# One loop of chunk pairs for all MLP passes, seven products in passes 2 to 4, Gelu in one ScalarE function, three raw weight buffers

## The chip, the core and the metric

The kernel runs on one core of a Trainium2 chip. TensorE multiplies into PSUM, VectorE (DVE in rows), ScalarE (ACT) and GpSimd (POOL) work on SBUF and PSUM, SyncE (SP) issues transfers. The metric is the time of one execution on the device in microseconds (us). A run's profile has a span, from the first to the last instruction; the time is a few us longer.

## What is computed

Clustered attention, then two MLP layers over its output, in float32 accuracy:

```python
mask = q_assign[:, :, :, None] == k_assign[:, :, None, :]
scores = np.where(mask, scale * np.matmul(q, k.transpose(0, 1, 3, 2)), -1000000000.0)
attn = softmax(scores)                      # B, H, S, D = 2, 8, 768, 64
x = np.matmul(attn, v).transpose(0, 2, 1, 3).reshape(B * S, H * D)     # 1536 x 512
h = x @ moe_w_in                            # layer 0: 512 -> 2048
x = (h * (1.0 / (1.0 + np.exp(-1.702 * h)))) @ moe_w_out
r = np.maximum(x @ moe2_w_in, 0.0)          # layer 1
out = (r * r) @ moe2_w_out
```

The weights come as float64 and are read as pairs of 32-bit words.

## The kernel before

Float32 products are made from two parts of each operand, a high part rounded to `F32R` and the rest as a low part; three products of parts (high by high, high by low, low by high) make one. A "part" step is a ScalarE copy to `F32R` and a subtract.

Attention comes first and isn't touched, apart from where decoded weights lie. Its end makes the parts `xs` of the first batch's rows and the hidden product of chunk 0.

The MLP runs in four passes: layer 0 on batch 0 and batch 1, layer 1 on batch 0 and batch 1. The 2048 hidden units are 16 chunks of 128 (`fc`). A chunk's hidden product has 24 matmuls, its second product (`second`, L719) adds into six PSUM tiles `y` and has 24 matmuls in layer 0 and 18 in layer 1, interleaved one chunk or pair later as `pend`.

- Pass 1 (L893 to L950) goes chunk by chunk, with 512 and 256 columns (`HALVES`). Within chunk `fc` it decodes the weights of chunk `fc + 1`: ScalarE takes the magnitude (`magnitude`, L81), VectorE does four steps (`decode`, L87: clamp, shift and mask, sign, low word), then ScalarE copies the high part and POOL subtracts the low one (`parts`, L105). The decoded first matrix is also stored to DRAM (`keep`, L123) for pass 2.
- Passes 2 to 4 (L960 to L1107) go by pairs of chunks, "slots" `q`. The first three slots of pass 2 (`NC = 3`) are plain: 48 matmuls of 384 columns for the hidden part. All others use seven products in place of eight, 42 matmuls (`product`, L836), with sums of rows (`Combos`) and of weights (`Weights.sums`). The weights are read back from DRAM two chunks at a time.
- In passes 2 and 3 the slots also decode layer 1's weights: `COUNTS` says how many tiles (of 32 `tasks`) a slot takes, `step` does one of five steps, `fetch` loads the next raw tile, `absolute` is the magnitude.
- Layer 0's activation is Sigmoid on ScalarE, a multiply on VectorE, a copy to the high part on ScalarE and a subtract on VectorE (`gate`, L701; `split`, L696; `low`, L712). Layer 1's is Relu and Square.
- The last slot of a pass makes five of seven parts of the next pass's rows (`nxt.part`), the first slot of a pass the other two, and empties `y` (`finish`).

The order on each engine is the order of the code (`manual_schedule`); a wait holds all that stands behind it on its engine. Raw weights have two buffers (`wraw`), decoded ones two (`tmpw`).

Of the kernel before, what the change touches and what calls it, by code (L numbers as in the profile page):

```python
# [34 lines left out]
def tile_kernel(ctx, tc, q, k, v, cent, w_in1, w_out1, w_in2, w_out2, cw_cols, out):  # L35
# [21 lines left out]
    wraw_p = ctx.enter_context(tc.tile_pool(name="wraw", bufs=2))  # L57
    tmp_p = ctx.enter_context(tc.tile_pool(name="tmpw", bufs=2))
# [13 lines left out]
    def w_dma(w, fc, first):  # L72
        raw = wraw_p.tile([P, DM, 2], U32, tag="raw64", name="raw64")
# [7 lines left out]
    def magnitude(raw):  # L81

        t = tmp_p.tile([P, raw.shape[1]], U32, tag="dec", name="dec")
        nc.scalar.activation(f32(t), f32(raw)[:, :, 1], ACTF.Abs)  # L84
        return raw, t
# [30 lines left out]
    def w_tiles(fc):  # L116

        wi = (wx_p if fc % 2 == 0 else wp_b[1]).tile([P, 2, KD * P], F32R, tag="wx", name="wi")
        return (wi[:, 0, :], wi[:, 1, :]) + out_tiles(fc)

# [13 lines left out]
    def hidden(xs, w, i, ph=None, span=slice(0, 3 * KD)):  # L134

        ih, il = w[0], w[1]
        a, n = HALVES[i]
        if ph is None:
            ph = duo.tile([P, n], F32, tag=("sd", "pt0")[i], name="ph")

        terms = [(w, kc, z) for w, z in ((ih, 0), (ih, 1), (il, 0)) for kc in range(KD)]
        for j, (w, kc, z) in list(enumerate(terms))[span]:
            nc.tensor.matmul(ph, w[:, kc * P:(kc + 1) * P], xs[kc][z][:, a:a + n],  # L143
# [4 lines left out]
    def attention(actx):  # L148
# [44 lines left out]
        raw = [w_dma(w_in1, 0, True), w_dma(w_out1, 0, False)]  # L193
# [332 lines left out]
        w1 = w_tiles(0)  # L526
# [28 lines left out]
        xs, mags = [], []  # L555
        none = lambda: None
# [33 lines left out]
        for t in range(-LEAD, NTILE):  # L590
# [43 lines left out]
            for i, at in enumerate((t + LEAD - GT, t + LEAD - 2 * GT, t + LEAD - 3 * GT, t + LEAD - 4 * GT)):  # L634
                fc, m = divmod(i, 2)
                if at == 0:
                    mags.append(magnitude(raw[m]))
                if 0 < at < 5:
                    decode(*mags[i], steps=(at - 1,), inside=i == 3)
                if at == 5:  # L640
# [15 lines left out]
        nc.scalar.activation(tiny.tile([P, 1], F32, name="warm", bufs=1), identF[:, 0:1], ACTF.Sigmoid)  # L656
# [3 lines left out]
        raw[0] = w_dma(w_in1, 3, True)  # L660
# [18 lines left out]
    xb_p = ctx.enter_context(tc.tile_pool(name="xb", bufs=6))  # L679
# [4 lines left out]
    NP = KF // 2  # L684
    h = m_p.tile([P, 2, S], F32, name="h")
    s = m_p.tile([P, S], F32, name="s")
    wt = m_p.tile([P, 4, 2 * P], F32, name="wt")
    p5 = m_p.tile([P, QB], F32, name="p5")
# [7 lines left out]
    def split(g, src, at=slice(0, S)):  # L696
        gh, gl = g
        nc.scalar.copy(gh[:, at], src[:, at])
        nc.vector.tensor_sub(gl[:, at], src[:, at], f32(gh[:, at]))
# [5 lines left out]
    def total(layer, dst, ps, other):  # L705

        if layer == 0:
            nc.vector.tensor_tensor(out=dst, in0=ps, in1=other, op=ALU.add)
        else:
            nc.vector._custom_dve(TENSOR_ADD_SAT, out=dst, in0=ps, in1=other, s0=TOP, s1=0.0)  # L710
# [4 lines left out]
    def squared(g, c, at):  # L715
        nc.scalar.activation(g[0][:, at], h[:, c, at], ACTF.Square)  # L716
        nc.scalar.activation(h[:, c, at], h[:, c, at], ACTF.Square)  # L717

    def second(layer, y, chunks):  # L719

        def unit(m, i):
            (gh, gl), (oh, ol), fc = chunks[i]
            if layer == 0:
                cs = slice(m * P, (m + 1) * P)
                yb = y[4 + m // 2][:, m % 2 * 256:m % 2 * 256 + 256]
                for z, (l, r) in enumerate(((oh, gl), (ol, gh), (oh, gh))):
                    first, last = fc == 0 and z == 0, fc == KF - 1 and z == 2
# [4 lines left out]
            else:  # L732
                for z, (l, r) in enumerate(((gh, oh), (gh, ol), (gl, oh))):
                    nc.tensor.matmul(y[m], l[:, m * P:(m + 1) * P], r,  # L734
                                     start=(fc == 0 and z == 0), stop=(fc == KF - 1 and z == 2))

        units = [(m, i) for m in range(6 if layer else KD) for i in range(len(chunks))]
# [3 lines left out]
    def finish(layer, y, b, k, copies=(nc.scalar.copy, nc.vector.tensor_copy)):  # L741
# [403 lines left out]
```

## Time and profile before

| | us |
|---|---|
| time, median of 3 runs | 802.42 (801.85 to 803.82) |
| profiled execution, its own time | 803.57 |
| its span | 800.6 |
| TensorE busy | 778.6 |
| VectorE busy | 645.2 |
| ScalarE busy | 507.5 |
| GpSimd busy | 163.7 |

Busy time is time with an instruction in the engine. Matmuls are pipelined: a matmul's listed time is longer than its distance to the next one, so pace is read from starts. A row of the timeline names its start, length, engine, line, operation, tiles out<-in, shape and count, and in brackets the idle time before it with what ended it.

### The profile page before, as it was taken

Reading aid. Unit: us, or ns where it says so; the run is one execution under the profiler, and the core shown is the slowest. Engines: PE = TensorE matmul, PEld = TensorE weight load, DVE = VectorE, ACT = ScalarE, POOL = GpSimd, SP = SyncE. Lnnn points to the kernel's source line nnn. Section 1 sums busy time; section 2 is a strip of 40 time slices with the busy share of each in tenths; the row PEclk is TensorE's granted clock in tenths of the full one; section 3 lists DMA queues with packets and bytes.
Section 4 is the critical chain, followed back from the end, with each engine's and each line's share of the span. In section 5 each row is a group of like instructions: output and inputs, shape, how many; then the busy total and the mean of one; then the engine's idle time right before and its main releaser. Section 6 shows DMA issues by size and latency. Waiting matters only on the chain.

```text
span 800.6 us, 12533 instructions
## 1 busy us (share of the span) xinstructions
PE 778.6 (97%) x4520; PEld 697.6 (87%) x4521; DVE 645.2 (81%) x1122; ACT 507.5 (63%) x1052; POOL 163.7 (20%) x153
## 2 busy tenths in 40 slices
PE   8999999999999999999989899999999999999997
PEld 5889989999989887788889799988999988898896
DVE  7899999998898799899879889988787887445532
ACT  5798888988978644454465554557565567445542
POOL 1435535545436234233300000000000000000000
PEclk9999999999999999999999999999999999999999
DMA  8242543532311344454546433321334301200002
GB/s 232 85 133 69 162 114 85 139 89 68 85 21 38 89 139 151 132 158 145 185 122 204 148 94 118 97 88 63 123 97 141 131 27 66 94 27 26 27 1 79
DMA packets 48477, 81.87 MB, mean 102 GB/s; under 512 B 5120, under 2 KB 32544, under 8 KB 48416
## 3 DMA queue, kind: packets, MB, share of 16 engines
q1 hardware_dynamic: 43232, 73.96, 30.8%
q10 hardware_dynamic: 5184, 7.12, 2.7%
q8 instruction: 35, 0.57, 0.3%
q14 instruction: 26, 0.21, 0.1%
HBM read 58.76 MB, written 11.58 MB: 88 GB/s over the span
## 4 chain that ended last, share of the span: by engine, by line
PE 58%; DVE 17%; DMA 12%; ACT 8%; issue 2%; POOL 1%; ACTq 0%; SPq 0%; POOLq 0%; DVEq 0%
PE ps L840 16%; PE y L734 15%; DMA raw<-in_moe_w_in_dram 6%; PE pa L456 5%; PE pt L431 5%; DMA raw<-in_moe_w_out_dram 3%; PE y L728 3%; PE ps L407 3%; DVE el L444 3%; PE ps L408 2%; DVE dec L98 2%; DVE nm L413 2%; DVE dec L101 2%; ACT dec L84 2%; DMA wst<-dec 2%
## 5 line engine op out<-in xcount | busy, mean ns | idle before, releaser
L444 DVE TENSOR_TENSOR el<-pt,eh 128x384 fp32r<-128x384 f32 x192 | 97.5, 549 | 8.0 <-ACT eh L441 7.4
L413 DVE TENSOR_REDUCE nm<-ps 128x1 f32<-128x768 f32 x96 | 91.2, 950 | 12.6 <-PE ps L408 11.8
L422 ACT ACTIVATE e<-ps,nm 128x768 f32<-128x768 f32 x96 | 88.7, 924 | 14.0 <-DVE rows L488 6.7
L441 ACT CAST eh<-pt 128x384 fp32r<-128x384 f32 x192 | 84.0, 497 | 9.9 <-PE pt L431 8.8
L431 PE MATMUL pt<-identF,e 128*128 128x128 f32 x576 | 81.8, 276 | 2.2 <-DVE el L444 1.6
L840 PE MATMUL ps<-x,wxh 128*128 128x384 f32 x336 | 73.6, 341 | 3.7 <-ACT wxh L812 2.7
L84 ACT ACTIVATE dec<-raw 128x512 f32<-128x512 f32 x64 | 43.1, 674 | 53.3 <-DMA raw<-in_moe_w_out_dram 27.1
L716 ACT ACTIVATE gh<-h 128x384 fp32r<-128x384 f32 (+1 forms) x48 | 30.4, 633 | 72.5 <-DVE h L710 72.0
L734 PE MATMUL y<-oh,gl 128*128 128x512 f32 x192 | 75.9, 395 | 0.0
L734 PE MATMUL y<-ol,gh 128*128 128x512 f32 x192 | 75.8, 395 | 0.0
L734 PE MATMUL y<-oh,gh 128*128 128x512 f32 x192 | 74.6, 389 | 0.0
L431 PEld LDWEIGHTS pt<-identF,e 128*128 128x128 f32 x576 | 64.4, 140 | 7.8 <-DVE el L444 6.9
L407 PE MATMUL ps<-k,q 80*128 80x512 f32 x192 | 70.2, 366 | 0.9 <-ACT k L374 0.5
L98 DVE SCALAR_TENSOR_TENSOR dec<-raw,dec 128x512 uint32<-128x512 uint32 x64 | 70.0, 1093 | 0.8
L713 DVE TENSOR_TENSOR gl<-h,gh 128x384 fp32r<-128x384 f32 (+1 forms) x75 | 50.0, 667 | 22.9 <-ACT h L717 19.6
L840 PEld LDWEIGHTS ps<-x,wxh 128*128 128x128 f32 x336 | 60.2, 191 | 7.7 <-ACT wxh L812 3.0
L408 PE MATMUL ps<-k,q 128*128 128x512 f32 x192 | 61.3, 340 | 0.0
L143 PE MATMUL ph<-xh,wi 128*128 128x512 f32 (+1 forms) x256 | 53.7, 342 | 3.7 <-ACT wi L107 3.4
L840 PE MATMUL ps<-x,wyh 128*128 128x384 f32 x252 | 54.7, 337 | 0.2 <-DVE x L791 0.2
L143 PEld LDWEIGHTS ph<-xh,wi 128*128 128x128 f32 x256 | 41.4, 189 | 12.1 <-ACT wi L107 6.5
L728 PE MATMUL y<-gl,oh 128*128 128x512 f32 x128 | 50.4, 394 | 0.9 <-DVE gl L713 0.9
L728 PE MATMUL y<-gh,ol 128*128 128x512 f32 x128 | 50.8, 397 | 0.0
(173 smaller groups left out, 1915.0 us busy)
## 6 DMA issues: line engine op xcount, KB each, us to landing
raw<-in_moe_w_in_dram SPq DMA_DIRECT2D x32, 512.0 KB, 4.0
raw<-in_moe_w_out_dram SPq DMA_DIRECT2D x32, 512.0 KB, 3.4
wb<-wst SPq DMA_DIRECT2D x24, 512.0 KB, 4.8
wst<-dec SPq DMA_DIRECT2D x32, 256.0 KB, 2.4
k<-k SPq DMA_DIRECT2D x16, 192.0 KB, 3.1
q<-q SPq DMA_DIRECT2D x16, 192.0 KB, 3.2
rr<-row SPq DMA_DIRECT2D x16, 192.0 KB, 3.5
out_dram<-o SPq DMA_DIRECT2D x12, 256.0 KB, 2.1
```

What stands on the lines that cost most here:

```text
L98: nc.vector.scalar_tensor_tensor(out=t, in0=high, scalar=0xC0000000, in1=t, op0=ALU.bitwise_and, op1=ALU.bitwise_or)
L143: nc.tensor.matmul(ph, w[:, kc * P:(kc + 1) * P], xs[kc][z][:, a:a + n], start=(j == 0), stop=(j == len(terms) - 1))
L407: nc.tensor.matmul(ps[:, a:a + n], q1[0:K1, qs], k1[0:K1, a:a + n], start=True, stop=False)
L408: nc.tensor.matmul(ps[:, a:a + n], q2[:, qs], k2[:, a:a + n], start=False, stop=True)
L413: nc.vector.tensor_reduce(out=nm, in_=live["s", t][:, 0:S], op=ALU.max, axis=AX, negate=True)
L422: nc.scalar.activation(e, live["s", t][:, 0:S], ACTF.Exp, bias=live.pop(("nm", t)), accum_out=sums[:, s:s + 1])
L431: nc.tensor.transpose(pt[:, i], e[:, kc * P:(kc + 1) * P], identF)
L441: nc.scalar.copy(place("eh", t, u), live["pt", t, u])
L444: nc.vector.tensor_tensor(out=place("el", t, u), in0=live.pop(("pt", t, u)), in1=f32(place("eh", t, u)), op=ALU.subtract)
L728: nc.tensor.matmul(y[m], l[:, cs], r[:, 0:512], start=first, stop=last)
L734: nc.tensor.matmul(y[m], l[:, m * P:(m + 1) * P], r, start=(fc == 0 and z == 0), stop=(fc == KF - 1 and z == 2))
L840: nc.tensor.matmul(ps, w[a][:, wi, kc * P:(kc + 1) * P], x[z][:, kc, :], start=start and j == kc == 0, stop=j == 2 and kc == 1, skip_group ...
```

## The change

- All passes run in one loop over 32 slots (layer, batch, pair). The eight slots of pass 1 are plain pairs (`PLAIN`) with two halves of 384 columns; slots 8 to 31 all use seven products. Slot 0 takes chunks 0 and 1, whose second hidden product stands in two `y` tiles.
- Layer 0's activation is `Gelu_apprx_sigmoid` on ScalarE, called twice, once into the high part and once into `h` (`active`); VectorE's multiply and the tiles `s` and `p5` are gone.
- The tasks now hold layer 0's remaining weights too (27 `near` tiles in pass 1), then layer 1's 32. Their subtracts are VectorE's; POOL has none of them any more. The magnitude may be taken one tile ahead in pass 1, into the weight tile of a later pair or into `room`.
- Raw weights have three buffers, taken in turn; the separate decoded tiles are gone. The last normalization (`last_norm`, on POOL) moves to the start of the MLP.
- The second product goes chunk by chunk within a pair (`order`), the later chunk first in passes 2 to 4, except in the last pair of a pass.

```diff
-    wraw_p = ctx.enter_context(tc.tile_pool(name="wraw", bufs=2))
-    tmp_p = ctx.enter_context(tc.tile_pool(name="tmpw", bufs=2))
+    wraw_p = ctx.enter_context(tc.tile_pool(name="wraw", bufs=1))
+    tmp_p = ctx.enter_context(tc.tile_pool(name="tmpw", bufs=1))
...
+    def raw_tile(at):
+        return (wraw_p, wraw_p, tmp_p)[at].tile([P, DM, 2], U32, tag=f"raw{at}", name="raw64")
...
-    def gate(dst, src, tmp):
-        nc.scalar.activation(tmp, src, ACTF.Sigmoid, scale=1.702)
-        nc.vector.tensor_mul(dst, src, tmp)
...
+    def active(layer, g, c, at, src=None):
+        if src is None:
+            src = h[:, c, at]
+        elif layer == 1:
+            nc.scalar.activation(h[:, c, at], src, ACTF.Relu)
+            src = h[:, c, at]
+        of = ACTF.Square if layer else ACTF.Gelu_apprx_sigmoid
+        nc.scalar.activation(g[0][:, at], src, of)
+        nc.scalar.activation(h[:, c, at], src, of)
...
-    NC = 3
-    COUNTS = (3, 4, 3, 2, 2, 2, 2, 0, 1, 2, 2, 2, 2, 2, 2, 1)
+    PLAIN = range(NP)
+    COUNTS = (2, 4, 4, 4, 4, 4, 4, 1) + (2, 3, 2, 2, 2, 2, 2, 1) + 8 * (2,)
+    EXTRA = {4: ((0, 0), (0, 1)), 5: ((0, 2), (0, 3)), 6: ((1, 0), (1, 1)), 7: ((1, 2), (1, 3))}
...
-    for fc in range(KF):
-        c = fc + 1
-        new = w_tiles(c) if c < KF else None
...
+        elif q in PLAIN:
+            extra = list(EXTRA.get(q, ()))
+            for c, g in ((0, ga), (1, gb)):
+                for i, at in enumerate((LO, HI)):
+                    u = 2 * c + i
+                    bank[i] = hidden(xs, wq.sides[c], i, bank[i] if not c else None)
+                    active(0, g, c, at, bank[i])
+                    if u:
+                        do(u - 1, (4,))
+                    if i:
+                        if q + 1 in PLAIN:
+                            wn.plain(c)
+                        else:
+                            wn.early(c)
+                    absolute()
+                    do(u, (0, 1))
+                    low(g, c, at)
+                    do(u, (2, 3))
+                    if i:
+                        before(2 * c)
+                        before(2 * c + 1)
...
+            if p == 0:
+                while len(x) < 7:
+                    combos.part(len(x))
```

On ScalarE within pass 1, before, one half-chunk after the other: `s` is the gate, `gh` a high part, `dec` a magnitude, `wi` the next chunk's weights.

```order
L702 ACTIVATE s<-ph 128x512
L84 ACTIVATE dec<-raw_4180 128x512
L698 CAST gh<-s 128x512
L702 ACTIVATE s<-ph 128x256
L107 CAST wi<-dec 128x512
L698 CAST gh<-s 128x256
```

The same place after, where `wxh` is the next pair's weights, `rr` is `room` and `wb` the weight tile of a later pair:

```order
L109 CAST oh<-rr 128x512
L806 CAST wxh<-wb 128x512
L86 ACTIVATE rr<-raw_4097 128x512
L708 ACTIVATE gh<-ph 128x384
L709 ACTIVATE h<-ph 128x384
L86 ACTIVATE wb<-raw_4126 128x512
```

The two calls that make `gh` and `h` now stand in a row, with nothing of VectorE between them. On VectorE in pass 1, before:

```order
L703 TENSOR_TENSOR s<-ph,s 128x512
L93 TENSOR_SCALAR dec<-dec 128x512
L95 TENSOR_SCALAR dec<-dec 128x512
L699 TENSOR_TENSOR gl<-s,gh 128x512
L703 TENSOR_TENSOR s<-ph,s 128x256
L98 SCALAR_TENSOR_TENSOR dec<-raw_4180,dec 128x512
L699 TENSOR_TENSOR gl<-s,gh 128x256
L101 SCALAR_TENSOR_TENSOR dec<-raw_4180,dec 128x512
```

and after, over half a chunk:

```order
L95 TENSOR_SCALAR rr<-rr 128x512
L97 TENSOR_SCALAR rr<-rr 128x512
L712 TENSOR_TENSOR gl<-h,gh 128x384
L100 SCALAR_TENSOR_TENSOR rr<-raw_4196,rr 128x512
L103 SCALAR_TENSOR_TENSOR rr<-raw_4196,rr 128x512
L110 TENSOR_TENSOR ol<-rr,oh 128x512
L807 TENSOR_TENSOR wxl<-wb,wxh 128x512
```

The multiplies `s<-ph,s` are gone, and the subtracts `ol` and `wxl`, which POOL had, have come. On VectorE at the end of pass 3, before, from the last pair's long low part to the first sum of pass 4:

```order
L713 TENSOR_TENSOR gl<-h,gh 128x768
L791 TENSOR_TENSOR x_7592<-x_0_85,x_7591 128x768
L813 TENSOR_TENSOR wxl<-wt,wxh 128x512
L713 TENSOR_TENSOR gl<-h,gh 128x384
L783 TENSOR_TENSOR x_0_85<-x_1_86,x_0_85 128x2x384
L791 TENSOR_TENSOR x_7588<-x_0_85,x_7587 128x768
L813 TENSOR_TENSOR wyl<-wt,wyh 128x512
L813 TENSOR_TENSOR wyl<-wb,wyh 128x256
L710 ISA h<-ps,p_5033 128x384
```

and after:

```order
L100 SCALAR_TENSOR_TENSOR room<-raw_7346,room 128x512
L712 TENSOR_TENSOR gl<-h,gh 128x768
L780 TENSOR_TENSOR xl<-x_0_85,xh 128x768
L103 SCALAR_TENSOR_TENSOR room<-raw_7346,room 128x512
L712 TENSOR_TENSOR gl<-h,gh 128x384
L807 TENSOR_TENSOR wxl<-wt,wxh 128x512
L110 TENSOR_TENSOR ol<-room,oh 128x512
L771 TENSOR_TENSOR x_0_85<-x_1_86,x_0_85 128x2x384
L780 TENSOR_TENSOR xl<-x_0_85,xh 128x768
L807 TENSOR_TENSOR wyl<-wt,wyh 128x512
L807 TENSOR_TENSOR wyl<-wb,wyh 128x256
L698 ISA h<-ps,h 128x384
```

A second tile's decode (`room`) and its subtract `ol` have come in between the parts of the next pass's rows.

## Rows read from the trace of the kernel before

**Rows 1.** Busy us (count) of PE, PEld, DVE, ACT, POOL; clock; DMA; GB/s.

```profile
274.80:402.80 128.00, 124.47 (x698) 106.71 (x697) 116.01 (x172) 61.43 (x118) 40.66 (x30) 1.00 0.49 152
402.80:533.50 130.70, 125.62 (x716) 117.68 (x715) 115.30 (x211) 70.32 (x133) 0.00 (x0) 0.99 0.41 129
533.50:661.60 128.10, 126.69 (x638) 113.42 (x637) 104.36 (x194) 79.61 (x147) 0.00 (x0) 1.00 0.27 91
661.60:800.60 139.00, 134.28 (x661) 119.59 (x659) 65.54 (x119) 66.21 (x123) 0.00 (x0) 1.00 0.13 46
```

**Rows 2.** Waits of TensorE in the MLP: us in total, times, longest.

```profile
PE ph L143 <- ACT wi L107: 3.4, 4, 1.5
PE ps L840 <- ACT wxh L812: 2.7, 1, 2.7
PE ps L847 <- DVE h L703: 2.4, 1, 2.4
PE y L728 <- DVE gl L713: 0.9, 1, 0.9
```

**Rows 3.** Timeline of TensorE, rows at which slots or their halves start.

```profile
274.78 0.40 PE L728 MATMUL y<-gl,oh 128*128 128x512 f32 x1
...
434.57 0.34 PE L847 MATMUL ps<-x,wxh 128*128 128x384 f32 x1
...
442.89 0.34 PE L847 MATMUL ps<-x,wxh 128*128 128x384 f32 x1
...
471.16 0.34 PE L840 MATMUL ps<-x,wxh 128*128 128x384 f32 x1
...
486.76 0.34 PE L840 MATMUL ps<-x,wxh 128*128 128x384 f32 x1
...
551.49 0.34 PE L840 MATMUL ps<-x,wxh 128*128 128x384 f32 x1
...
567.17 0.33 PE L840 MATMUL ps<-x,wxh 128*128 128x384 f32 x1
...
772.49 0.33 PE L840 MATMUL ps<-x,wxh 128*128 128x384 f32 x1
```

**Rows 4.** VectorE groups of 287:400, then 551:645 (busy, mean ns | idle); then timeline.

```profile
L98 DVE SCALAR_TENSOR_TENSOR dec<-raw,dec 128x512 uint32<-128x512 uint32 x25 | 41.1, 1643 | 0.4
...
L98 DVE SCALAR_TENSOR_TENSOR dec<-raw,dec 128x512 uint32<-128x512 uint32 x12 | 8.3, 689 | 0.2
L101 DVE SCALAR_TENSOR_TENSOR dec<-raw,dec 128x512 uint32<-128x512 uint32 x12 | 8.3, 688 | 0.2
L95 DVE TENSOR_SCALAR dec<-dec 128x512 uint32<-128x512 uint32 x12 | 5.1, 427 | 0.4
...
L813 DVE TENSOR_TENSOR wxl<-wb,wxh 128x512 fp32r<-128x512 f32 x6 | 4.2, 693 | 4.6 <-ACT wxh L812 4.6
...
300.82 2.29 POOL L504 TENSOR_TENSOR x<-x,rr 128x768 f32<-128x768 f32 x1
301.44 2.22 DVE L101 SCALAR_TENSOR_TENSOR dec<-raw,dec 128x512 uint32<-128x512 uint32 x1
```

**Rows 5.** ScalarE groups of 287:400, pass 1.

```profile
L84 ACT ACTIVATE dec<-raw 128x512 f32<-128x512 f32 x24 | 16.2, 674 | 45.8 <-DMA raw<-in_moe_w_out_dram 24.6 <-DMA raw<-in_moe_w_in_dram 21.2
...
L702 ACT ACTIVATE s<-ph 128x512 f32<-128x512 f32 (+1 forms) x26 | 12.6, 486 | 0.0
```

**Rows 6.** A stretch of 3 us behind the 2.7 us wait, columns as in Rows 1.

```profile
454.00:457.00 3.00, 2.91 (x9) 2.92 (x10) 3.00 (x6) 2.70 (x7) 0.00 (x0) 0.50 0.98 337
```

**Rows 7.** Timeline of VectorE and TensorE at the seam of passes 3 and 4.

```profile
660.59 0.96 DVE L713 TENSOR_TENSOR gl<-h,gh 128x768 fp32r<-128x768 f32 x1 [0.34 <-ACT h L717]
...
663.75 0.39 PE L734 MATMUL y<-oh,gh 128*128 128x512 f32 x1
...
667.08 0.55 DVE L710 CUSTOM_DVE_ANT_0 h<-ps,p 128x384 f32<-128x384 f32 x1
...
667.68 0.44 PE L840 MATMUL ps<-x,wxh 128*128 128x384 f32 x1 [0.63 <-DVE h L710]
```

More of the change, by code (lines that the diff above doesn't have):

```diff
@@ L951, in tile_kernel @@
-    weights[0, 0].plain(0)
-    for i in (7, 6):
-        combos.part(i)
-    weights[0, 0].plain(1, weights[0, 0].x)
-    p1, u2 = tmp12[:, 0:QB], tmp12[:, QB:S]
-    slots = [(layer, b, p) for layer, b in ((0, 1), (1, 0), (1, 1)) for p in range(NP)]
-    ends = (0, y, 0)
+        layer, kind, fc = tasks[n]
+        t = ready[n][1]
+        if k < 4:
+            decode(*ready[n], steps=(k,))
+        if k == 4 and kind == 0:
+            keep(layer, fc, f32(t))
+        if k == 3 + (kind == 0):
+            fetch()
@@ L960, in tile_kernel @@
+    fetch()
+    fetch()
+    slots = [(layer, b, p) for layer in range(2) for b in range(B) for p in range(NP)]
+    nxt = None
+    at_bank = 0
+    ends = None
     for q, (layer, b, p) in enumerate(slots):
-        bank = [duo.tile([P, QB], F32, tag=("sd", "pt0")[(q + i) % 2], name="ps") for i in range(2)]
+        bank = first if q == 0 else [
+            duo.tile([P, QB], F32, tag=("sd", "pt0")[(at_bank + i) % 2], name="ps") for i in range(2)]
         A, B_ = bank
-        if p == 0 and q:
+        n = COUNTS[q] if q < len(COUNTS) else 0
+        more = q + 1 < len(slots)
+        last = p == NP - 1 and more
+        if p == 0:
@@ L1009, in tile_kernel @@
-                    do(u, (4,))
-            wo = wo1
-            if p == 0:
-                y = y_tiles()
-            pend = second(layer, y, [(ga, wo.get(2 * p), 2 * p), (gb, wo.get(2 * p + 1), 2 * p + 1)])
-            ends = (layer, y, b)
-            continue
-        last = p == NP - 1 and q + 1 < len(slots)
-        more = q + 1 < len(slots)
-        product(A, wq.x, wq.B11, x[Combos.A11], True)
-        wq.late()
-        if q == NC:
-            combos.part(3)
-        nc.scalar.copy(p1, A)
@@ new lines, in tile_kernel @@
+            low(gb, 1, ALL)
+            if last:
+                nxt.part(3)
+            before(2)
+            product(A, wq.y, wq.T4, x[Combos.A22])
+            active(layer, ga, 0, HI, A)
+            if more and n < 2:
+                wn.early(1)
+            if n > 1:
+                do(end, (3,))
+            low(ga, 0, HI)
+            if more and n > 1:
+                wn.early(1)
+            if n > 1:
+                do(end, (4,))
+            if q < 3 * NP and p > 3:
+                nxt.sum(p - 4)
@@ L1104, in tile_kernel @@
+            if last:
+                nxt.part(4)
+            before(3)
+        if p == 0 and q:
             y = y_tiles()
[L1105 to L1106 removed]
+        pend = second(layer, y, [(g, 2 * p + i) for i, g in enumerate((ga, gb))],
+                      None if p == NP - 1 else (0, 1) if q in PLAIN else (1, 0))
         ends = (layer, y, b)
```

439 lines of the change are left out of this document (181 added, 258 removed).

## Prediction

> **What bounds the kernel now.** I read the busy time by stage first. In each of the four MLP passes TensorE is busy 96 to 99% of its stretch, and VectorE 91, 88, 81 and 47% [rows 1]. So the end is set by TensorE: its work, plus its idle time. I then read what TensorE waited for in the MLP [rows 2]: 3.4 us on the ScalarE copy of `wi` in pass 1, 2.4 us on the gate's VectorE multiply (`h L703`) at the start of pass 2, 2.7 us on `wxh` where pass 2 goes over to seven products, and 0.9 us on `gl` at the seam of passes 2 and 3. Idle time is not all that is lost, so third I read the starts of slots (one pair of chunks) [rows 3]. An undisturbed half of a plain pair takes 442.89 - 434.57 = 8.32 us, a pair 16.64. An undisturbed seven-product pair takes 486.76 - 471.16 = 15.60 us in layer 0 and 567.17 - 551.49 = 15.68 in layer 1; I use 15.70. Against these, pass 1 from its first `y` matmul at 274.78 took 128.0 us, and pass 2 took 130.7 [rows 1, 3].
>
> **The sum, on TensorE's clock of slots.** The changed order starts pair 1 where the first `y` matmul stood (the hidden part of chunk 1 still goes before it, with as many columns). Then come 7 plain pairs, 8 seven-product pairs of layer 0, and 15 of layer 1 until the last pair starts: 274.8 + 7 x 16.64 + 8 x 15.60 + 15 x 15.70 = 751.6 us. Before, the last pair started at 772.5 [rows 3]; what follows it, to the end of the span at 800.6, is the same. So 20.9 us go if nothing new waits. The parts of this, roughly: 3 x 1.04 = 3.1 us for the 18 matmuls that three pairs lose; 7.3 us in pass 1 (128.0, against 116.5 for 14 chunks and 4.2, half of 8.32, for one chunk's second product); 7 us of waits in pass 2; 3.4 at the seams of passes 2/3 and 3/4.
>
> **Pass 1.** Why the waits on `wi` go: before, each chunk's weights are decoded, copied and subtracted in the chunk ahead, and POOL's subtract blocks VectorE. `L98` takes 1.64 us on average there, 0.69 in passes 3 and 4 where POOL is silent; one `L101` under POOL's norm took 2.22 [rows 4]. After, POOL keeps only that one norm, and VectorE takes over the subtracts. Its work in a plain pair with four tiles to decode: 4 low parts at 0.55 (the 384-wide row in [rows 7]) = 2.2; 2 weight subtracts at 0.69 = 1.4; 4 decodes of 0.43 + 0.43 + 0.69 + 0.69 = 2.24 (both short steps by `L95`'s row) = 9.0; 2 subtracts for `ol` = 1.4 [rows 4]. That is 13.9 us, and 15.8 in pairs 4 to 6, which carry two 768-wide sums or parts more, at 0.96 (the 768-wide row in [rows 7]). Both lie under 16.64, and the order leaves slack: a pair's weights are ready over 10 us ahead of TensorE, a low part some 6 us ahead. The multiplies of the gate are gone. So I price this work at nothing; TensorE's 16.64 us hide it, and if that cover goes the excess is paid pair by pair (a rival below).
>
> **One function on ScalarE.** Gelu isn't in the trace. Its nearest rows are Sigmoid out of PSUM, 0.49 us at this mean width, and the Abs over 512 elements, 0.67 [rows 5]. I take 0.49, since it is the same instruction with another table. ScalarE's plain pair: 8 x 0.49 = 3.9, 4 Abs 2.7, 4 copies at no more than an Abs 2.7, two 768-wide copies at no more than two Abs each 2.7: at most 12.0 of 16.64. It would bind only at (16.64 - 8.1) / 8 = 1.07 us per Gelu. Below 0.49 nothing is gained, as TensorE doesn't wait for it. The compiled order holds three table loads before and after, so none is added. In product pairs the chain from product to low part loses one VectorE step, which removes the waits on `h L703`.
>
> **Three raw buffers.** ScalarE's idle time before the Abs was spent on raw weights, yet no wait of TensorE names a transfer [rows 2]. I price the third buffer at nothing. The cover is ScalarE's spare 4.6 us a pair; SP has the same transfers and stores queued in the same order of need, and one raw tile now has two tiles' time to land.
>
> **Pass 2 without plain pairs.** The switch to seven products moves to the seam of passes 1 and 2. There the first two weight blocks are made half a pair ahead, so the 2.7 us wait goes. With it goes its echo: the granted clock stood at its lower level (0.50, which is 1.2 GHz) in the 3 us behind that wait, after TensorE had stood idle, and at 2.4 GHz elsewhere [rows 6]. At half the clock 3 us of work lose about 1.5; this is in the 20.9. The first product pair holds three 768-wide parts, two decodes and two copies of `y`: on VectorE about 16 us, beside 15.60. It starts without a backlog, since the pair before it has one decode. I allow 0.5 us.
>
> **New waits.** Passes 2 and 3 now decode 16 tiles each, and the last pair of pass 3 decodes two where it had one. It also makes five parts for pass 4 there. Before, VectorE was already 3.3 us behind in this place: TensorE was through the second product at 663.75, VectorE reached its sum at 667.08, and the product that needs the bank waited 0.63 us for it [rows 7]. One more tile is 2.24 + 0.69 = 2.9 us of VectorE. VectorE also idled there, 0.34 us in one row of [rows 7], and the second tile can fill such pieces, so the backlog grows by 2.1 to 2.6, and some of it is paid earlier, at the fifth product. I take 2.5 us of waits in place of 0.63; the bounds are 0.6 (idle time takes it all) and 5 (it is paid in full and stops the next low parts too). At the seam of passes 2 and 3 one tile (2.9) is added and three multiplies (about 2.0) go: 0.5, where 2.2 were lost. The start of the MLP, where POOL's norm blocks one VectorE step by about 2.3 us: 0.5. Sum of new waits: 0.5 + 2.5 + 0.5 + 0.5 = 4.0, with bounds 1 and 10.
>
> **Total.** Span 800.6 - 20.9 + 4.0 = 783.7. The profiled execution took 803.57, 2.97 more than its span: 786.7. It lay 1.15 above the median of 802.42, so I predict a median of 785.5 us.
>
> **Rivals.**
> *The backlog is paid with the clock.* The waits at the end of pass 3 or in the first product pair come in one piece as long as the 2.7 us that was followed by the lower clock. Price: 2 to 5 us more idle and 1.5 for each such piece: 789 to 795. For it: with 2.9 us more, VectorE has more work in that last pair than TensorE's 15.7 us, and it came to its end 3.3 us late before. Against it: the backlog is paid at three places, each under 1 us by my sum. Chance 0.17.
> *Part of pass 1 stays on VectorE.* `L98` stays at 1.64 for a reason other than POOL. That adds 4 x 0.95 = 3.8 us a pair, so 17.7 (pairs 1 to 3) and 19.6 us against 16.64: 12 us in all, hence 797.5 with the rest as above. Against it: `L101` of the same shape is 0.69 except under POOL [rows 4]. The Trainium skill (SBUF — State Buffer, Who interferes with whom) says the two engines' common ports are an exclusive lock for a whole instruction. By that rule the added 0.95 us goes with POOL and this case falls away; the trace agrees, 2.22 us beside POOL's 2.29. Chance 0.04.
> *VectorE becomes the bound of pass 1, slower than before.* As the last, but `L101` also costs its longest, 2.22. Then a pair takes 23.8 to 25.7 us of VectorE: about 49 us more, 834. The point from which it decides: a decoded tile must cost 1.2 us more than 2.24, since 785.5 becomes 804.8 when six pairs each take 3.2 us more than 16.64. Against it is the same row. Chance 0.04.
> *The seven products don't pay.* Pass 2's three pairs gain nothing because VectorE is late in all of them, and pass 1's waits turn into waits at the seams: only half of 20.9 comes, and the new waits stay: 796. Chance 0.04.
> *Nothing new waits.* 781.5, or a little less. Chance 0.06.
>
> **How the numbers follow.** The forecast, 782.5 to 789, has 0.65; the rest as given. The range 780.5 to 795 leaves out the three rivals above 795 (0.12) and the ends of the bounds, about 2 in 10 with what I haven't thought of. About 0.3% can be told from no change here: below 800.0 is faster, above 804.8 slower. Faster: 0.65 + 0.17 + 0.04 + 0.04 + 0.06 less a few hundredths for errors of the sum = 0.92; same 0.04; slower 0.04.
>
> **What would show it.** Right: in pass 1 of the changed trace no wait of TensorE above 0.3 us and pairs 16.6 us apart; the shift-and-mask step of the decode at 0.69; no lower clock around the seam of passes 1 and 2; eight layer-0 pairs 15.6 apart; a wait on the sum `h` in the first pair of pass 4 of some 2 us in pieces. Wrong: pairs of 18 us or more in pass 1, Gelu far above 0.49 us, table loads beyond three, or TensorE waiting for raw weights through ScalarE's Abs.

## The result and the profile after

The changed kernel takes 783.99 us (median of 4 runs, 783.74 to 785.25), the kernel before, run beside it, 802.13 us (801.36 to 803.82). The ratio is 0.9774, with an interval of 0.9755 to 0.9793: 18.1 us less. The profiled execution took 784.22 us, its span is 782.4. The prediction was 785.5, from 780.5 to 795.

First the page of the changed kernel: its span, the busy time of each engine, and the clock that TensorE was granted in 40 slices (9 is 90% or more; its mean was 1.000).

```profile
span 782.4 us, 12369 instructions
...
PE 769.3 (98%) x4502; PEld 700.7 (90%) x4503; DVE 617.3 (79%) x1118; ACT 509.3 (65%) x1058; POOL 122.4 (16%) x123
...
PEclk9999999999999999999999999999999999999999
```

Then two windows, the plain pairs of pass 1 and the product pairs from pass 2 to the first of pass 3, with the columns of [rows 1], and everything that TensorE waited for in the MLP (us in total, times, longest), which answers to [rows 2].

```profile
278.36:391.68 113.32, 112.66 (x650) 105.47 (x650) 92.97 (x172) 57.92 (x116) 0.00 (x0) 1.00 0.52 165
391.68:532.20 140.52, 140.52 (x813) 131.64 (x812) 119.16 (x222) 84.77 (x156) 0.00 (x0) 1.00 0.36 115
```

```profile
PE ps L837 <- DVE h L698: 1.4, 2, 0.7
PE ph L138 <- ACT h L709: 0.7, 1, 0.7
```

Four groups of waits, 9.4 us in [rows 2], and 1.1 us in three smaller waits have become three waits of 2.1 us. TensorE is busy 140.52 of 140.52 us in the second window. Last, its timeline at the starts that answer to [rows 3], with the idle time ahead of a row in brackets.

```profile
278.36 0.39 PE L725 MATMUL y<-gl,oh 128*128 128x512 f32 x1
...
365.72 0.34 PE L138 MATMUL ph<-xh,wxh 128*128 128x384 f32 x1
...
383.18 0.44 PE L138 MATMUL ph<-xh,wxh 128*128 128x384 f32 x1 [0.66 <-ACT h L709]
...
391.68 0.34 PE L837 MATMUL ps<-xh,wxh 128*128 128x384 f32 x1
...
407.28 0.33 PE L837 MATMUL ps<-xh,wxh 128*128 128x384 f32 x1
...
532.20 0.34 PE L837 MATMUL ps<-xh,wxh 128*128 128x384 f32 x1
...
639.87 0.44 PE L837 MATMUL ps<-xh,wyh 128*128 128x384 f32 x1 [0.73 <-DVE h L698]
...
649.56 0.44 PE L837 MATMUL ps<-xh,wxh 128*128 128x384 f32 x1 [0.66 <-DVE h L698]
...
754.65 0.33 PE L837 MATMUL ps<-xh,wxh 128*128 128x384 f32 x1
```

From 278.36 to 365.72 TensorE runs 87.36 us without a gap: 5.25 plain pairs of 16.64. The hidden part at 383.18 would have started at 382.36, and the product pairs at 390.68 in place of 391.68; that is the one disturbance of pass 1, in pair 7 (pair 1 starts at 274.20, pair 7 at 374.04, its second chunk's hidden part is the row at 383.18). The first product pair takes 407.28 - 391.68 = 15.60; nine pairs up to 532.20 take 140.52, which is 8 x 15.60 + 15.72, so there was nearly nothing at the seam of passes 2 and 3. From 532.20 the 14 pairs of layer 1 up to the last pair's start take 222.45 us against 14 x 15.70 = 219.8: 2.6 us at the seam of passes 3 and 4, around the two waits at 639.87 and 649.56.

Gelu, which was priced from Sigmoid's row, and the decode's slow step, in pass 1 (275 to 391 us; busy us, mean ns; compare [rows 4, 5]):

```profile
L708 ACT ACTIVATE gh<-ph 128x384 fp32r<-128x384 f32 x14 | 6.8, 484 | 0.0
...
L100 DVE SCALAR_TENSOR_TENSOR rr<-raw,rr 128x512 uint32<-128x512 uint32 x14 | 9.6, 685 | 0.0
```

Gelu takes 0.48 us, the shift-and-mask step 0.69.

### The profile page after: what moved, and what is told of

The parts are those of the page before. It is cut to its first block, busy times and chain, and to the rows that moved or that the text cites. A ratio compares the mean times of both kernels' runs of the same rounds, so it can differ in the third digit from the quotient of the medians.

```text
span 782.4 us, 12369 instructions
## 1 busy us (share of the span) xinstructions
PE 769.3 (98%) x4502; PEld 700.7 (90%) x4503; DVE 617.3 (79%) x1118; ACT 509.3 (65%) x1058; POOL 122.4 (16%) x123
## 4 chain that ended last, share of the span: by engine, by line
PE 61%; DVE 3%; ACT 1%; issue 0%; DVEq 0%
PE ps L837 21%; PE y L731 16%; PE y L725 10%; PE y L727 5%; PE ph L138 4%; PE ps L138 3%; DVE xl L780 1%; PE y L138 1%; DVE gl L712 0%; PE pa L451 0%; DVE ol L110 0%; DVE wyl L807 0%; DVE h L698 0%; DVE wxl L807 0%; ACT gh L708 0%
## 5 line engine op out<-in xcount | busy, mean ns | idle before, releaser
L708 ACT ACTIVATE gh<-h 128x384 fp32r<-128x384 f32 (+1 forms) x64 | 41.4, 647 | 101.1 <-DVE h L698 71.1
L712 DVE TENSOR_TENSOR gl<-h,gh 128x384 fp32r<-128x384 f32 (+1 forms) x104 | 67.1, 646 | 19.7 <-ACT h L709 19.5
L807 DVE TENSOR_TENSOR wxl<-wb,wxh 128x512 fp32r<-128x512 f32 x37 | 25.5, 690 | 40.3 <-ACT wxh L806 40.2
L725 PE MATMUL y<-gh,oh 128*128 128x512 f32 x128 | 50.1, 391 | 0.0
L837 PE MATMUL ps<-xh,wxh 128*128 128x384 f32 x192 | 48.9, 336 | 0.7 <-DVE h L698 0.7
L837 PE MATMUL ps<-xl,wxh 128*128 128x384 f32 x192 | 49.3, 337 | 0.0
L451 PE MATMUL pa<-eh,v 128*128 128x384 f32 x192 | 49.1, 365 | 0.1
L837 PE MATMUL ps<-xh,wxl 128*128 128x384 f32 x192 | 49.1, 336 | 0.0
L698 DVE CUSTOM_DVE_ANT_0 h<-ps,h 128x384 f32<-128x384 f32 x48 | 26.4, 556 | 24.1 <-PE ps L837 23.4
```

Source lines behind the costliest of these rows:

```text
L712: nc.vector.tensor_sub(g[1][:, at], h[:, c, at], f32(g[0][:, at]))
L725: nc.tensor.matmul(y[m], l[:, cs], r[:, 0:512], start=first, stop=last)
L837: nc.tensor.matmul(ps, w[a][:, wi, kc * P:(kc + 1) * P], x[z][kc], start=start and j == kc == 0, stop=j == 2 and kc == 1, skip_group_check ...
```

## Experiments

The first question was which part of the change the 18 us belong to; the forecast had given the gain of pass 1 to POOL's silence and had priced the third raw buffer at nothing. The second was the new wait that the forecast didn't have (pair 7), the third the price of the seam and of the clock. Times are medians, ratios are to the kernel before on the same chip.

**One function, put into the kernel before.** The multiply goes, ScalarE writes Gelu (here the lines of `gate`; the product pairs, not shown, are changed alike):

```
-        nc.scalar.activation(tmp, src, ACTF.Sigmoid, scale=1.702)
-        nc.vector.tensor_mul(dst, src, tmp)
+        nc.scalar.activation(dst, src, ACTF.Gelu_apprx_sigmoid)
```

> The kernel before with only the one function: Gelu on ScalarE in place of Sigmoid and VectorE's multiply; the copy and all else stay. Theory: 2.4 us of waits on the multiply at the start of pass 2 go, VectorE gets back 14 us of pass 1's 113, and the waits on wi (3.4 us) shrink, while the shift-and-mask step stays at 1.64 under POOL: 4 to 8 us less, 794 to 798. Rival (pass 1 of before is held by the POOL-bound chain from raw tile to wi and not by VectorE's amount of work): only pass 2 gains, 799 to 801.

> The kernel before with the one function in all of layer 0 (the run e4_before_one_function left the second chunk's multiply in the five product pairs, by a factor that was left over, so its output was not the reference's). Expected like that run, 794.0, or up to 2 us less, since the seam of passes 2 and 3 loses one VectorE step of 0.95 us there: 792 to 794.5. Rival (those multiplies were hidden): 794 within 0.5.

The first of the two left the multiply of the second chunk in the five product pairs, by a stale factor. It took 794.04 us, the full one 794.19 (ratio 0.9879, 0.9856 to 0.9901): some 9 us less than before. Between the two no price of those five multiplies can be read. In the profiled execution of the full run 2.2 us of the gain lie in pass 1, which took 125.8 us in place of 128.0. TensorE's waits in the full run:

```profile
PE ps L839 <- DVE wxl L812: 1.8, 1, 1.8
PE ph L143 <- ACT wi L107: 1.6, 2, 1.3
PE ps L839 <- DVE h L709: 0.6, 1, 0.6
PE ps L846 <- ACT h L702: 0.3, 1, 0.3
```

Against [rows 2], the 2.4 us on the multiply are 0.3, the 0.9 us on `gl` are gone, the 3.4 us on `wi` have halved though POOL still works there.

**VectorE's subtracts, put into the kernel before, alone and with the function.** The four calls of `parts` in pass 1 get VectorE as their engine:

```
-            parts(tf, new[0], new[1])
+            parts(tf, new[0], new[1], nc.vector)
```

> The kernel before with one part of the change: the weights' low parts of pass 1 subtracted by VectorE in place of POOL. Theory P (as the prediction had it: POOL's subtracts make the weights late): the shift-and-mask step falls from 1.64 to 0.69 us, 24 us of VectorE go and 18 come, the waits on wi go, pass 1 (15 y blocks and 14 hidden blocks, 122.1 us undisturbed) falls from 128.0 to 122 to 123.5: 796.5 to 798. Rival L (the chunk loop makes a chunk's weights only one chunk ahead, through one chain from raw tile to Abs, four decode steps, copy and subtract, so that they are late whatever POOL does; what cured pass 1 is the longer lead): the step falls to 0.69 all the same, but pass 1 stays above 126: 800 to 803.

> The kernel before with both: the one function and VectorE's subtracts in pass 1; chunk loop, lead, two raw buffers and plain pairs of pass 2 stay. If POOL and the multiply together held pass 1 (theory P), it takes 122 to 123 us, 3 to 4 less than with the one function alone (126.2): 789 to 791. If the lead held it (rival L): still 125 to 127, 793 to 795.

Alone: 802.85 us over 10 runs, ratio 0.9998 (0.9983 to 1.0013). No gain can be read, though VectorE's groups show the block gone:

```profile
L98 DVE SCALAR_TENSOR_TENSOR dec<-raw,dec 128x512 uint32<-128x512 uint32 x25 | 17.2, 687 | 0.4
```

This step gave VectorE 24 us back, and the subtracts took 17 of them; its busy time in pass 1 fell from 116.0 to 104.8 us. The profiled execution was the fastest of the ten (span 798.2): in it the waits on `wi` were 1.5 us in place of 3.4, and pass 1 took 126.1 us in place of 128.0. The ten runs together show nothing of that. Theory P falls as a cause by itself. With the function: 791.55 us (0.9853, 0.9835 to 0.9870), and pass 1 takes 124.6. So the subtracts are worth 2 to 3 us once the multiply is gone (the intervals of the two runs overlap a little), and the function 9 alone and 11 beside them.

6 to 8 us are left from there to the changed kernel. TensorE's starts in the two profiled executions say where, with one chunk's second product (4.16 us) counted to the same pass in both: of 7.2 us up to the last pair's start, 5.5 lie in pass 2 (3.1 for the matmuls that three pairs lose, the rest mainly around the switch from plain pairs to products, whose wait was still 1.5 us in this run), 2.9 in pass 1 and 0.4 ahead of it, and 1.6 are lost again in passes 3 and 4. Of the 2.9, 1.4 are no wait: TensorE's undisturbed chunk takes 8.42 us in pass 1 before and 8.32 after. So 1.5 us at most are left for the weights made a pair ahead, beside the function and the subtracts; that lead was not tried singly.

**POOL's subtracts, put back into the changed kernel.**

```
-                parts(f32(t), *wo[layer, fc], nc.vector)
+                parts(f32(t), *wo[layer, fc], nc.gpsimd if q < NP else nc.vector)
```

and the same for `wxl` in `Weights.part`.

> The changed kernel with the weights' low parts of pass 1 (ol and wxl) subtracted by POOL again, as before. Theory (POOL's subtracts block VectorE's two-input step, no other reason): the shift-and-mask step of the decode goes from 0.69 to about 1.64 us in pass 1, the subtracts take 1.3 to 1.45 us on POOL; VectorE's pair is 13.9 - 2.8 + 3.8 = 14.9 us in pairs 1 to 3 and 16.8 in pairs 4 to 6, so pass 1 gets longer by 1 to 5 us: 785 to 789, with waits of TensorE in slots 4 to 7. Rival (the step was slow for another reason, such as the raw tile or the buffers it writes): the step stays at 0.69 and the time is that of the changed kernel within 0.5 us.

786.02 us (0.9783, 0.9764 to 0.9803), 2 us more than the changed kernel by the medians, 1 by the ratios, whose intervals overlap. Groups of VectorE and POOL and the waits of TensorE in it:

```profile
L100 DVE SCALAR_TENSOR_TENSOR wb<-raw,wb 128x512 uint32<-128x512 uint32 x11 | 16.3, 1482 | 0.0
...
L100 DVE SCALAR_TENSOR_TENSOR rr<-raw,rr 128x512 uint32<-128x512 uint32 x14 | 9.6, 685 | 0.0
...
L807 POOL TENSOR_TENSOR wxl<-wb,wxh 128x512 fp32r<-128x512 f32 x14 | 20.9, 1490 | 19.6 <-ACT wxh L806 19.6
...
PE ps L138 <- POOL wxl L807: 1.4, 1, 1.4
```

The steps of one kind of tile are blocked to 1.48 us, as long as a POOL subtract (1.49); those of the other, which fall between the subtracts, take 0.69. That is one more row for the rule that the forecast took from the Trainium skill (SBUF — State Buffer, Who interferes with whom), and it agrees. But the plain pairs stay at 16.64 us: the one wait that POOL adds is 1.4 us at the very start. With weights made a pair ahead, the block is hidden.

**The multiply, put back into the changed kernel.**

```
+            nc.scalar.activation(tmp, src, ACTF.Sigmoid, scale=1.702)
+            nc.vector.tensor_mul(h[:, c, at], src, f32(tmp) if src_is_h else tmp)
+            nc.scalar.copy(g[0][:, at], h[:, c, at])
```

> The changed kernel with layer 0's activation as before: Sigmoid on ScalarE, multiply on VectorE, copy on ScalarE (in the product pairs the sigmoid factor is kept in the low operand's tile, rounded to that type, so the output is less exact). Theory (the one function matters because VectorE would else be the bound): VectorE gets 2.2 us more per plain pair, 16.1 in pairs 1 to 3 and 18.0 in pairs 4 to 6 against TensorE's 16.64, and 2.05 us more per product pair of layer 0, some 16.3 against 15.60. So pairs 1 to 3 stay near 16.6, pairs 4 to 6 take about 18, product pairs of pass 2 about 16.3: 4 + 6 = 10 us more, 792 to 797. Rival (the multiply lies beside TensorE's work and costs only where a low part waits for it, as the sum priced it): 784 to 787, all pairs within 0.2 us of their undisturbed lengths.

> As e1_multiply_back, but ScalarE copies the hidden part out of its PSUM bank first, so that the bank waits for ScalarE alone, and VectorE multiplies in SBUF (the sigmoid factor is kept in the low operand's tile, rounded to that type, so the output is less exact). In e1_multiply_back TensorE waited 20 us for the multiply, by name, to give a bank back. Theory B (the held bank is the price): those waits go, pairs of pass 1 fall from 17.8 to 20 us to 16.7 to 17.2, the time from 818.7 to 788 to 800. Rival V (VectorE itself is the bound: in that run's pass 1 it was busy 82 of 100 us and stood 16.5 us of the rest behind ScalarE's copies, so each pair needs some 18 to 20 us of it wherever the bank is given back): TensorE waits elsewhere, on gl or h, and the time stays over 808.

818.66 us (1.0190, 1.0166 to 1.0215): some 34 us more than the changed kernel, and slower than before. Theory and rival of its expectation were both far too low. The pairs of pass 1 take 17.83 us and 19.56, counted from the hidden part of pair 2's and of pair 5's second chunk to the next pair's. First these two windows, then, from the changed kernel, those of the same pairs (columns as in [rows 1]), then what ScalarE and VectorE waited for in 285 to 391 us of the run with the multiply, and last a wait of ScalarE in the changed kernel's pass 1:

```profile
302.96:320.79 17.83, 17.12 (x99) 15.56 (x97) 14.63 (x29) 8.16 (x17) 0.00 (x0) 1.00 0.48 148
358.27:377.83 19.56, 17.46 (x98) 15.56 (x97) 16.36 (x31) 8.16 (x17) 0.00 (x0) 1.00 0.42 134
```

```profile
299.16:315.80 16.64, 16.64 (x99) 15.67 (x98) 12.78 (x25) 7.91 (x16) 0.00 (x0) 1.00 0.49 158
349.08:365.72 16.64, 16.64 (x99) 15.67 (x98) 14.43 (x27) 8.22 (x17) 0.00 (x0) 1.00 0.49 158
```

```profile
ACT gh L712 <- DVE h L711: 51.4, 22, 3.8
...
DVE ol L110 <- ACT oh L109: 12.1, 11, 1.1
DVE wxl L814 <- ACT wxh L813: 4.4, 6, 0.7
...
ACT wxh L806 <- PE ph L138: 11.1, 6, 2.2
```

VectorE is busy 14.63 of 17.83 us and 16.36 of 19.56: both times 3.2 us of a pair are not busy, and for 2.9 of them it stands behind ScalarE's copies, as ScalarE stands 51 us behind VectorE's multiply. So a pair of VectorE costs its busy time and some 3 us of round trips with ScalarE in this run. In the changed kernel VectorE waits on ScalarE's copies as well, but most of that is no round trip: 10.8 us of it, between 285 and 385 us, are for `wxl`, behind a copy `wxh` that itself waits for TensorE to give a weight tile back (the last line). There VectorE is early, and at 12.8 to 14.4 us busy its pairs fit under 16.64. The second run tells the held PSUM bank from this: ScalarE copies the bank out first, and the multiply reads SBUF. It took 812.62 us (1.0115, 1.0091 to 1.0140), 6 us less, with pairs of 17.0 and 18.8 us in these places, so rival V holds for most of the price and the bank for a part; TensorE then waited for ScalarE's `h` instead. The added copy is work for ScalarE too, so the bank's part may be more than 6 us. In the run with the multiply as it was, the product pairs of pass 2 took part in the loss: 135.5 us against 124.8.

**Two raw buffers in the changed kernel.**

```
-            fetched.append(w_dma(((w_in1, w_out1), (w_in2, w_out2))[layer][kind], fc, kind == 0, n % 3))
+            fetched.append(w_dma(((w_in1, w_out1), (w_in2, w_out2))[layer][kind], fc, kind == 0, n % 2))
```

> The changed kernel with its raw tiles in two buffers in turn in place of three. Theory (as priced: the third buffer is worth nothing on the path): ScalarE's Abs waits for raw weights rise from 8.6 us in pass 1 to 30 to 50 us, but no wait of TensorE names them; 784 within 1 us. Rival (ScalarE works in order, so a late Abs holds the Gelu behind it): a tile's transfer takes 4.2 us and with two buffers starts a tile later, so hidden parts' Gelus come late by 1 to 2 us in many half pairs: 788 to 800, with waits of TensorE on ScalarE's h or VectorE's gl in pass 1.

837.05 us (1.0425, 1.0406 to 1.0444): some 53 us more, far over the rival's 800. ScalarE's timeline in pass 1 shows how:

```profile
298.24 0.66 ACT L86 ACTIVATE wb<-raw 128x512 f32<-128x512 f32 x1 [6.49 <-DMA raw<-in_moe_w_in_dram]
298.80 0.48 ACT L708 ACTIVATE gh<-ph 128x384 fp32r<-128x384 f32 x1
```

The Abs waits 6.49 us for a transfer, and the Gelu, whose bank TensorE wants, stands behind it: 59.4 us of ScalarE's waits between 285 and 391 us are on these transfers. The next run keeps two buffers and issues an Abs only when the tile before it is decoded:

```
-        if n < len(tasks) and n < len(fetched) and 5 * n <= len(steps) + 5:
+        if n < len(tasks) and n < len(fetched) and 5 * n <= len(steps):
```

> As e3_two_raw (two raw tiles in turn), and the Abs of a tile is issued only when the tile before it is decoded. Theory (with two buffers the 53 us came from ScalarE's order: the early Abs waited for a transfer of 4.2 us that had only just started, and the Gelu stood behind it): the waits of ScalarE on raw weights fall from over 59 us in pass 1 to 5 to 25, and the time to 786 to 800. Rival (two buffers cannot feed a tile each 4.16 us, wherever the Abs stands): over 820.

805.54 us (1.0030, 1.0014 to 1.0046). It lies between theory and rival, and neither had the reason. Pass 1 now runs as in the changed kernel, with 16.64 us a pair: two buffers do feed it, and the early Abs was the price there. The 20 us that stay are at the seam of passes 2 and 3 and in pass 3. What TensorE waited for, what ScalarE and the queue of SP waited for between 520 and 680 us, and two issues of that queue:

```profile
PE ps L837 <- DVE h L698: 11.4, 9, 1.9
PE ps L837 <- DVE h L696: 3.9, 1, 3.9
...
ACT wxh L806 <- DMA wb<-wst: 28.5, 7, 4.6
...
SPq L81 <- DVE room L103: 94.1, 10, 19.0
...
547.98 0.38 SPq L78 DMA_DIRECT2D raw<-in_moe_w_in_dram  x1
548.40 0.51 SPq L792 DMA_DIRECT2D wb<-wst  x1
```

The load of the decoded weights (`wb`, L792) needs no raw buffer, but it stands in SP's order behind a raw transfer (L78, L81) that waits until VectorE's last decode step has given a raw tile back: its own buffer was free by 545.2 us, it was issued at 548.40, and ScalarE's copy stood until 553.47. VectorE stands behind such copies for 33.5 us in these 160 us, and TensorE behind VectorE's sum. In the changed kernel SP waits 37.9 us in place of 94.1 for that step, and ScalarE has no wait on `wb` between 535 and 640 us. The later Abs isn't the cause here: the run with two buffers and the early Abs has the same waits in these passes, 29.3 us of ScalarE on `wb`, 11.7 and 4.0 of TensorE on `h`. So the third buffer carries two things at once: an Abs a tile ahead, and an SP queue that stands less.

**The seam of passes 3 and 4, and pair 7.** One decoded tile moves from the last pair of pass 3 to its second pair; in the second run pass 2's operand sums and parts also come one pair earlier, so that pair 6 has none:

```
-    COUNTS = (2, 4, 4, 4, 4, 4, 4, 1) + (2, 3, 2, 2, 2, 2, 2, 1) + 8 * (2,)
+    COUNTS = (2, 4, 4, 4, 4, 4, 4, 1) + (2, 3, 2, 2, 2, 2, 2, 1) + (2, 3, 2, 2, 2, 2, 2, 1)
...
-    EXTRA = {4: ((0, 0), (0, 1)), 5: ((0, 2), (0, 3)), 6: ((1, 0), (1, 1)), 7: ((1, 2), (1, 3))}
+    EXTRA = {3: ((0, 0), (0, 1)), 4: ((0, 2), (0, 3)), 5: ((1, 0), (1, 1)), 7: ((1, 2), (1, 3))}
```

> The changed kernel with one decoded tile moved from the last pair of pass 3 to its second pair. Theory (the 2.5 us at the seam of passes 3 and 4 are VectorE's backlog from that tile): the waits on the sum h in pass 4's first pair fall from 0.7 and 0.7 us to one of 0.6 or none, the seam loses 0.3 to 1.2 us in place of 2.5: 782.0 to 783.0 against 784.0. Rival (the backlog is the five 768-wide parts of pass 4 and the copies of y, not the tile): the seam still loses over 2 us, 783.7 to 784.3; or the third tile in the second pair brings a new wait there.

> As e9_seam, and the sums and parts of pass 2's operands moved one pair earlier, so that pair 6 of pass 1 carries none and pair 7 two. Theory (the wait of 0.66 us in pair 7, on ScalarE's h, is VectorE's backlog from pair 6: four tiles and two parts there are 15.8 us of VectorE, ScalarE's oh copy waits for it, and the Gelu stands behind that copy): pairs 1 to 7 all take 16.64 us, another 1.0 us goes: 781 to 782. Rival (the wait comes from pair 7's own order): it stays, 782 to 783.

The first: 784.15 us (0.9770, 0.9755 to 0.9785), no difference that can be measured. In its trace the wait of 0.73 us is gone and the one of 0.66 is still 0.65; about 0.5 us are lost anew in the second pair, where the third tile now is. The second: 782.82 us (0.9751, 0.9736 to 0.9765). Its timeline of TensorE at the hidden part of pair 7, at the seam and at the last pair's start:

```profile
382.26 0.41 PE L138 MATMUL ph<-xh,wxh 128*128 128x384 f32 x1
...
648.03 0.62 PE L837 MATMUL ps<-xh,wxh 128*128 128x384 f32 x2 [0.66 <-DVE h L698]
...
753.12 0.33 PE L837 MATMUL ps<-xh,wxh 128*128 128x384 f32 x1
```

The wait in pair 7 is gone, and the last pair starts 1.5 us earlier than in the changed kernel (0.3 of it ahead of pair 1). Of all runs this is the fastest by its median, 1.2 us under the changed kernel, though the two intervals overlap. So VectorE's work in pair 6 makes the wait of pair 7, as the theory says; its way to TensorE stands in the changed kernel's timeline:

```profile
378.31 0.68 ACT L86 ACTIVATE rr<-raw 128x512 f32<-128x512 f32 x1 [0.23 <-DVE ol L110]
...
381.01 0.69 DVE L103 SCALAR_TENSOR_TENSOR rr<-raw,rr 128x512 uint32<-128x512 uint32 x1
...
381.74 0.62 ACT L109 CAST oh<-rr 128x512 fp32r<-128x512 f32 x1 [2.75 <-DVE rr L103]
382.26 0.48 ACT L708 ACTIVATE gh<-ps 128x384 fp32r<-128x384 f32 x1
382.65 0.48 ACT L709 ACTIVATE h<-ps 128x384 f32<-128x384 f32 x1
```

The late decode step holds ScalarE's copy of `oh`, the Gelu stands behind the copy, and TensorE behind the Gelu. But it is no backlog that grows from pair to pair. VectorE falls 0.9 us back in pair 4, with the first two of pass 2's sums, and then keeps step: the last low part of pairs 4 and 5 starts at 346.31 and 362.95, 16.64 us apart, and pairs 5 and 6 have the same 14.4 us of work. What is special to pair 6 is its last tile. In pairs 1 to 5 the fourth tile belongs to the first matrix and needs no copy on ScalarE; pair 6's belongs to the second, like the third before it. Both use `room`, so its Abs waits for the third tile's subtract (the first row), its four steps follow one after the other, and its `oh` stands ahead of pair 7's first Gelu. In pair 6 that Gelu (362.25) follows the Abs (361.67) at once; in pair 7 it comes 3.95 us behind it. In the run without parts in pair 6 the same chain stands 0.96 us earlier, and that is enough.

**Doses of idle work.** VectorE gets extra steps ahead of its sum in four pairs of pass 4:

```
+            for _ in range({25: 6, 27: 8, 29: 10, 30: 12}.get(q, 0)):
+                nc.vector.tensor_tensor(out=room, in0=room, in1=room, op=ALU.add)
             total(layer, 0, LO, B_)
```

> The changed kernel with idle work on VectorE in pass 4, ahead of its sum at the second product: 6, 8, 10 and 12 two-input steps of 512 elements (0.69 us each: 4.1, 5.5, 6.9 and 8.3 us) in pairs 2, 4, 6 and 7 of the pass. Theory: the sum has about 3.6 us of slack until TensorE wants its bank for the fourth product, so TensorE waits 0.5 to 1, 2 to 2.5, 3.3 to 4 and 4.7 to 5.3 us there, each in one piece; behind the waits of 2.7 us and more the granted clock falls to 0.50 for about 3.4 us, as in the kernel before, and costs 1.5 us each; behind the shorter ones it stays. Time 784 + 11 to 13 of waits + 3 to 4 of clock: 797 to 801. Rival (the length of one wait does not decide the clock): the clock stays at 1.00 behind a wait over 2.7 us, or falls behind a shorter one.

809.74 us, one run. TensorE's rows behind the four doses, and windows around its restart after the first and the last (length, busy PE, clock, DMA share, GB/s):

```profile
669.27 0.75 PE L837 MATMUL ps<-xh,wxh 128*128 128x384 f32 x2 [2.30 <-DVE h L698]
...
705.67 0.62 PE L837 MATMUL ps<-xh,wxh 128*128 128x384 f32 x2 [3.16 <-DVE h L698]
...
743.50 1.01 PE L837 MATMUL ps<-xh,wxh 128*128 128x384 f32 x2 [4.62 <-DVE h L698]
...
767.64 1.01 PE L837 MATMUL ps<-xh,wxh 128*128 128x384 f32 x2 [6.07 <-DVE h L698]
```

```profile
669.60:673.00 3.40, 3.40 (x11) 0.50 0.00 0
...
765.20:772.00 6.80, 4.36 (x12) 0.50 0.00 0
```

Waits of 2.3, 3.2, 4.6 and 6.1 us are 16.1 together; the run lost 25.7 against the changed kernel. Of the rest, 1.1 us was lost before the MLP's first pair (it starts at 275.34 in place of 274.20). The four dosed stretches of TensorE are 4.1, 5.0, 7.0 and 8.3 us longer than the same stretch of a pair without a dose (4.19 us), so 8.2 us are left beside the waits: 1.8, 1.8, 2.4 and 2.2. They went with the lower level of the clock (0.50, 1.2 GHz) behind each of the four, some 2 us for each piece, not 1.5. Behind the two short waits it lasted about 3.4 us; at the two long ones 6.8, of which the first 2.2 to 2.4 still lay in the wait. The slack ahead of the sum is some 2.6 us (10 steps took 7.2 us and gave 4.62 of wait), not 3.6.

## Why the prediction came out, step by step

- **The frame held.** TensorE's slots set the end: plain pairs at 16.64, layer 0's product pairs at 15.60, layer 1's at 15.70. The last pair was put at 751.6 + 4.0 = 755.6 and started at 754.65. The profiled execution was 784.22 against 786.7 by the sum: 1.0 of the 2.5 us is the last pair's start (pair 1 started at 274.20, not 274.8, and the new waits were 0.3 less), 0.3 the span behind it, and 1.2 that this execution lay 1.82 us over its span where that of before lay 2.97 over.
- **New waits, 4.0 by the sum, were 3.7, and in other places.** The seam of passes 3 and 4 was put at 2.5 and lost 2.6, in pieces under 1 us as forecast. Its cause was sized wrongly: with the extra tile gone, 1.4 of the 2.6 stay, so the tile explains less than half. The start of the MLP and the first product pair lost nothing (0.5 each by the sum), the seam of passes 2 and 3 lost 0.1 in place of 0.5. Pair 7 lost 1.0 that the text didn't have.
- **"I price this work at nothing" failed in pair 7.** The sum counted VectorE's instructions (15.8 us in pairs 4 to 6; measured 14.4) and held them against 16.64. As an amount that cover holds: pairs 4 to 6 lost nothing. It left out the order: the last tile of pair 6 is decoded one step after another, and its copy stands ahead of a Gelu on ScalarE. Two parts of pass 2's operands in the same pair made this chain about 1 us too late.
- **"Why the waits on `wi` go" named a part of the cause.** The shift-and-mask step fell to 0.69 as forecast (its row for POOL's silence is from pass 3 alone, not from passes 3 and 4). But POOL's silence put into the kernel before gave no gain that ten runs show, and 2 to 3 us beside the function; POOL's subtracts put back into the changed kernel left its pairs at 16.64. What the runs show beside it is the one function, some 9 us by itself and 2.2 of them in pass 1, and at most 1.5 us for the order that makes weights a pair ahead. Of the 7.3 us counted for pass 1, 1.4 are no wait at all: before, an undisturbed chunk took 8.42 us (4.18 for the hidden part, 4.24 for the second product), after 8.32 (4.16 for each). The second product has blocks of 512 and 256 columns in both, so the new halves of 384 don't explain it; its cause stays open.
- **"Below 0.49 nothing is gained" and "the multiplies are gone" under-sized the function.** Gelu took 0.48 us. The gain is not in ScalarE's time but in VectorE's step and its round trip: without the function this order costs 34 us more.
- **"I price the third buffer at nothing" failed.** It gives no gain that can be read as one, which is why the total came out; but the order rests on it. The cover that the text named, ScalarE's spare 4.6 us a pair, is no cover: with two buffers 53 us are lost, or 20 with a later Abs. The reason offered, that no wait of TensorE names a transfer, only tells of an order in which no Abs runs ahead.
- **The clock's echo went, as forecast:** the granted clock is full from the first slice to the last. The rival that the backlog is paid with the clock didn't come; its price of 1.5 us a piece was too low, by the doses 1.8 to 2.4.
- The rivals of VectorE as the bound of pass 1 and of products that don't pay didn't come. The first was nearer than 0.04 says: one more VectorE step per low part, in the run with the multiply, makes the kernel slower than before.

So the sum was right because TensorE had nothing left to wait for, and any mix of reasons that covers all waits gives the same number. The reasons were right in part only, and the total couldn't tell: that it came so near is in part luck.

## What to carry to other kernels

An amount of work that fits under a period isn't yet hidden: VectorE at 14.4 us busy in a period of 16.64 kept its period, and one decode step, 1 us late ahead of a ScalarE copy, still held the Gelu and TensorE. So ask of each step whose order its result stands in. Where two engines hand tiles to and fro, count their round trips too: with the multiply VectorE needed 3.2 us a pair beside its busy time. Before a part is priced at nothing, ask what else in the new order leans on it: a buffer that saves no wait today may be what lets an early instruction, or a queue that issues in order, run on. And undo each part singly before believing where a gain came from: here VectorE's subtracts gained nothing alone and 2 to 3 us beside the function, and the function 9 us in the old order and 34 in the new.

## What the runs showed of the hardware that was not expected

- The length of one wait doesn't decide whether TensorE's clock falls behind it. In the run with the one function a wait of 1.81 us was followed by 3.3 us at 0.50; in the run with two raw buffers one of 2.92 us was followed by full clock, and one of 2.87 us (up to 321.48) by 3.4 us at 0.50; and in the run with the multiply one of 2.81 by full clock. Windows behind the waits of 1.81, 2.92 and 2.81 us (the second starts within its wait):

```profile
449.60:452.90 3.30, 3.30 (x12) 0.50 0.92 336
...
341.00:346.00 5.00, 2.77 (x15) 1.00 0.44 163
...
403.30:408.00 4.70, 4.68 (x27) 1.00 0.33 106
```

- One load in SP's queue that waited for a buffer stopped loads behind it that had all they needed: 28.5 us of ScalarE's waits on `wb` in the run with two buffers and the later Abs, against none on it between 535 and 640 us in the changed kernel.
